# Attention and a gated long convolution on one core: scores of four heads per product, and values multiplied in 64-row halves

## The chip, the cores and the metric

The kernel runs on one core of a Trainium2 chip. The metric is the device time of one execution in microseconds; the median of the runs shown is compared. In the profile PE is TensorE (PEld its weight loads), DVE is VectorE, ACT is ScalarE, POOL is GpSimd and SP is SyncE, which here only issues transfers. Lines such as L691 are lines of the kernel before, unless the text says otherwise.

## What is computed

Eight batches, twelve heads, 448 positions, 64 features per head. Attention whose softmax has one more term in its denominator, then a projection into three parts, a circular convolution of the second part along the positions, a product of the three, and an output projection:

```python
scores = q @ k.T / sqrt(64)                     # per batch and head, 448 x 448
m = max(scores); e = exp(scores - m)
attn = e / (sum(e) + exp(-m) + 1e-09)           # the same as exp(s) / (sum(exp(s)) + 1)
x = (attn @ v).transpose(0, 2, 1, 3).reshape(8, 448, 768)
proj = x @ w_proj; x1, x2, x3 = three parts of 768
x2_conv = irfft(rfft(x2, axis=1) * rfft(filter, axis=0))
out = (x1 * x2_conv * x3) @ w_out               # 8 x 448 x 768, float32
```

All inputs are float32; the kernel multiplies in bf16 and sums in float32.

## The kernel before

**Two kinds of work.** For each batch there is attention (six pairs of heads) and then `dense(b)`: folding of x (`first`, `second`), the projection of the convolved part (`proj2`, L865), its spectrum by a small matrix of sines and cosines (`spectrum`, L892), the product with the filter's spectrum on VectorE (L906, L912), the two gates (`gate`, L938), the inverse transform (`inverse`, L977), unfolding and gating on VectorE, and the output projection (`project`, L1050). Attention of later batches is run between the pieces of dense work of earlier ones.

**An order made by a planner.** Nothing is emitted where it is written. Every piece is a task, added with an engine, a cost, a due time, what it needs, makes, takes and gives back. `Plan.run` imitates the engines and writes the tasks out in the order in which they would start; each engine then runs its own part of that order strictly in sequence. The due times come from the tables ATT, SLOT, DENSE, PACE, FOLD, LEAD, LOAD and others, so other tables give another order on every queue. The eight banks of PSUM are given out in the same way ("sc" and "op" take two neighbours, "hy" one). Where the plan leaves TensorE idle between 3 and 36 us it puts in filler products of zeros (L1136).

**Loads.** Four heads (a group, 24 in all) arrive together. `load_rows` (L372) reads keys or queries of four heads into 128 partitions: 64 partitions for each of two heads, seven successive positions in each partition, two such pairs beside each other. Values are read by `load_values` (L382) in four pieces of 64 partitions, so that two different blocks of seven stand under each other. `cast_rows` (L388) and `cast_values` (L393) turn them to bf16, on GpSimd save for the first group. The first two batches (`staged`) are transposed on TensorE (L437) and copied out of PSUM (L442); later ones (`loaded`) are transposed by a DMA on SP's queue (L483), keys and queries each by their own. There are six float32 rooms at first, then five.

**Scores and exponentials.** The 448 keys of a head are seven blocks of 64. A score task (`scores`, L655) makes four products, 64 keys by 448 queries on one quarter of the array each. For t = 1, 2, 3 the four are blocks t-1 and t+3 of two heads, so that one exponential (L666, 128 x 896) holds 128 keys of each head. Block 3 is left over; t = 0 puts block 3 of all four heads into one product, whose exponential goes into one of two buffers `er`; the other three use a ring of six buffers `e`. The first scores are single, then two are run together (`run`).

**Values.** The sum over keys for a pair of heads has two parts: `out_rests` (L683), eight products over 64 rows for block 3, and `out_rest` (L691), twelve products over 128 rows for each head. A column of ones beside the values gives the denominator. `out_rests` of pair j is emitted in the score run of the next pair. `norm` (L704 to L706) divides on VectorE and writes `xb`; `xb` is transposed to `xT` on TensorE in batch 0 (L779, L786, L788) and by DMA from batch 1 on (L770), four pairs and then two.

**Weights.** w_proj comes in on GpSimd's queue in its three parts (L631; the middle part in halves), the filter at L547 to L551, w_out at L636. They are asked for between the casts, in the planner's order.

The layout that the value products depend on:

```python
x = w_ if t else u ^ c                # which head's columns
j = t - 1 + 4 * c if t else 3         # which block of keys, on half c of the rows
```

## Time and profile before

| | |
|---|---|
| median of three runs | 393.48 us (392.73 to 393.92) |
| the profiled execution, by the timer | 388.91 us |
| its span in the profile | 387.1 us |
| TensorE granted clock, mean | 0.995 |
| scores, L655 | 672 products, 50.6 us busy |
| values over 128 rows, L691 | 1152 products, 44.6 us busy |
| values over 64 rows, L683 | 384 products, 14.2 us busy |
| gates, L938 | 576 products, 123.8 us busy |
| exponentials, L666 | 168, 147.7 us busy |
| SP's queue: value loads, L382 | 96, median 0.61 us to issue |

Busy time of a group is the union of its instructions; since a product takes some 0.19 us from start to end and the next starts long before that, the mean duration of one is not its price. The price is the distance between starts. The profiled execution's span stands below the median of the runs by 6.4 us, so sums are made against the span.

### The profile page before, as it was taken

The page shows a single profiled execution, that of the slowest core. Times are in us where ns is not written, and L with a number is a line of the kernel's source. Part 1 is how long each engine was busy: PE and PEld are TensorE (multiplying, and loading weights), DVE is VectorE, ACT ScalarE, POOL GpSimd, SP SyncE. Part 2 cuts the span into 40 slices and gives each one's busy share as a digit, 9 for nine tenths or more (in the row PEclk, how much of TensorE's full clock was granted, in tenths as well). Part 3 has the DMA queues.
Part 4 walks back from the last instruction along what each step waited for, and adds up shares of the span by engine and source line. Part 5 has one row for each costly group of instructions (what it writes and reads, how often), then busy time and mean ns, then how long its engine had stood idle before and what let it go on. Part 6 is the DMA issues. An engine that isn't in the chain of part 4 may idle for free.

```text
span 387.1 us, 9875 instructions
## 1 busy us (share of the span) xinstructions
PE 371.2 (96%) x3988; PEld 227.0 (59%) x3988; DVE 265.3 (69%) x651; ACT 263.7 (68%) x436; POOL 78.0 (20%) x97
## 2 busy tenths in 40 slices
PE   7989999999799999999999999999999999999995
PEld 4656755546555575555755456556665666657552
DVE  7388477893878838994489824986279745796480
ACT  4888777856756768866687576776677568634543
POOL 3832513140622323232222210000000000000000
PEclk9999999999989999999999999999999999999999
DMA  8999999999998999999988765220321012410204
GB/s 247 266 267 251 245 258 236 186 242 274 299 200 176 314 232 265 196 269 263 270 202 184 124 194 109 47 29 2 129 51 30 0 42 67 112 27 3 117 8 163
DMA packets 90862, 63.86 MB, mean 165 GB/s; under 512 B 58365, under 2 KB 87232, under 8 KB 90816
## 3 DMA queue, kind: packets, MB, share of 16 engines
q1 hardware_dynamic: 86064, 57.36, 59.6%
q0 software_dynamic: 4480, 5.41, 8.0%
q8 instruction: 31, 0.51, 0.5%
q10 hardware_dynamic: 272, 0.46, 0.3%
q14 instruction: 15, 0.12, 0.1%
HBM read 43.86 MB, written 11.01 MB: 142 GB/s over the span
## 4 chain that ended last, share of the span: by engine, by line
PE 74%; DVE 16%; DMA 6%; issue 2%; ACT 1%; POOL 0%; DVEq 0%
PE psum L938 22%; PE psum L865 16%; PE psum L1050 13%; PE psum L691 8%; PE psum L655 8%; DVE t L906 3%; DMA filt<-in_moe_filter_fft_dram 3%; PE psum L892 2%; PE psum L977 2%; PE psum L683 2%; DMA xT<-xb 2%; DVE xb L706 1%; DVE yh L912 1%; DVE g L953 1%; DMA nat<-in_q_dram 1%
## 5 line engine op out<-in xcount | busy, mean ns | idle before, releaser
L666 ACT ACTIVATE e<-psum 128x896 bf16<-128x896 f32 x144 | 125.7, 921 | 21.3 <-PE psum L655 20.7
L938 PE MATMUL psum<-xT,wproj_bf 128*128 128x448 bf16 x576 | 123.8, 355 | 0.1
L938 PEld LDWEIGHTS <-wproj_bf 128*128 128x128 bf16 x576 | 53.4, 98 | 46.3 <-issue 6.2
L865 PE MATMUL psum<-wproj_bf,xf 128*113 128x384 bf16 x384 | 70.2, 327 | 0.0
L865 PEld LDWEIGHTS <-xf 128*113 128x113 bf16 x384 | 49.2, 132 | 13.2 <-issue 1.4
L1050 PE MATMUL psum<-wout_bf,yT 128*128 128x384 bf16 x288 | 52.1, 326 | 2.4 <-DVE yT L1021 1.3
L655 PE MATMUL psum<-qT,kT 64*64 64x448 bf16 x672 | 50.6, 364 | 0.8 <-DVE xb L706 0.7
L953 DVE TENSOR_TENSOR g<-x,psum 128x448 bf16<-128x448 bf16 x48 | 29.5, 615 | 24.8 <-PE psum L938 24.6
L691 PE MATMUL psum<-vn,e 128*128 128x65 bf16 x1152 | 44.6, 194 | 0.0
L950 ACT CAST x<-psum 128x448 bf16<-128x448 f32 x48 | 25.7, 535 | 26.0 <-PE psum L938 25.6
L1062 ACT COPY osb<-psum 128x384 f32<-128x384 f32 x56 | 26.0, 484 | 22.2 <-PE psum L1050 21.8
L691 PEld LDWEIGHTS <-e 128*128 128x128 bf16 x1152 | 39.0, 97 | 2.7
L906 DVE TENSOR_TENSOR t<-xs,hrs 113x768 bf16<-113x768 bf16 (+1 forms) x64 | 37.4, 625 | 3.8 <-ACT xs L900 3.8
L1050 PEld LDWEIGHTS <-yT 128*128 128x128 bf16 x288 | 26.8, 98 | 22.1 <-issue 3.1
L704 DVE TENSOR_SCALAR rec<-psum 128x8 f32<-128x8 f32 x48 | 7.8, 162 | 39.4 <-PE psum L691 38.6
L706 DVE TENSOR_TENSOR xb<-psum,rec 128x512 bf16<-128x512 f32 x48 | 33.2, 691 | 1.7
L877 DVE CAST x<-psum 113x384 bf16<-113x384 f32 x32 | 17.7, 554 | 23.9 <-PE psum L865 23.8
L900 ACT CAST xs<-psum 113x384 bf16<-113x384 f32 (+1 forms) x64 | 28.2, 493 | 6.4 <-PE psum L892 5.8
L986 ACT CAST cr<-psum 128x452 bf16<-128x452 f32 x48 | 25.5, 548 | 9.1 <-PE psum L977 8.9
L388 POOL CAST nat<-nat 128x896 bf16<-128x896 f32 x22 | 22.6, 1028 | 41.2 <-DMA nat<-in_q_dram 17.4
L393 POOL CAST vn<-nat 128x896 bf16<-128x896 f32 x17 | 16.2, 954 | 71.9 <-DMA nat<-in_v_dram 56.6
L879 ACT CAST x<-psum 113x384 bf16<-113x384 f32 x32 | 15.4, 487 | 22.3 <-PE psum L865 22.3
(97 smaller groups left out, 381.0 us busy)
## 6 DMA issues: line engine op xcount, KB each, us to landing
out_dram<-osb SPq DMA_DIRECT2D x24, 384.0 KB, 2.6
nat<-in_k_dram SPq DMA_DIRECT2D x17, 448.0 KB, 4.9
nat<-in_q_dram SPq DMA_DIRECT2D x16, 448.0 KB, 5.5
nat<-in_v_dram SPq DMA_DIRECT2D x34, 128.0 KB, 4.6
nat<-in_v_dram SPq DMA_DIRECT2D x34, 96.0 KB, 4.5
wproj_bf<-in_moe_w_proj_dram POOLq DMA_DIRECT2D x2, 1152.0 KB, 15.5
k<-in_k_dram SPq DMA_DIRECT2D x4, 448.0 KB, 5.3
q<-in_q_dram SPq DMA_DIRECT2D x4, 448.0 KB, 5.2
```

Of the source, the lines that this page charges most:

```text
L655: nc.tensor.matmul(sc[64 * c : 64 * c + 64, u, 0:S], kT[b % 2][r, g, j, 64 * x : 64 * x + 64], qT[b % 2][r, g, :, 64 * x : 64 * x + 64],)
L666: nc.scalar.activation(e[:, 0 : 2 * S].rearrange("p (u n j) -> p u n j", u=2, j=7), pair(("sc", ("S", i, t)))[:, :, 0:S].rearrange("p u (j ...
L691: nc.tensor.matmul(out_bank(u)[:, n, :], P["e"][1 + t][:, u * S + n * 128 : u * S + n * 128 + 128], vn[b % 2][:, 2 * g + u, 4 * (u ^ w_) + ...
L706: nc.vector.tensor_tensor(W["xb", b][:, 2 * g : 2 * g + 2, :, 64 * w_ : 64 * w_ + 64], op[:, :, :, 0:DH], rec[:].unsqueeze(3).to_broadcast ...
L865: nc.tensor.matmul(pps[:FQ, :DCH], W["xf", b][:, pg, kt, 0:FQ], wproj_bf[:, kt, D + ch * DCH : D + (ch + 1) * DCH], start=(kt == 0), stop= ...
L900: nc.scalar.copy(L["xs", par, ch][:K, pg % 2, :], L["Z", pg, ch][:K, :DCH])
L906: nc.vector.tensor_tensor(t[:K], L["xs", par, ch][:K], h, op=ALU.mult)
L938: nc.tensor.matmul(p[:, :S], wproj_bf[:, kt, 2 * part * D + dt * 128 : 2 * part * D + (dt + 1) * 128], xT()[:, kt, 0:S], start=(kt == 0), ...
L950: nc.scalar.copy(L["x1", dt], p[:, :S])
L953: nc.vector.tensor_tensor(g[:, dt, :], L["x1", dt], p[:, :S], op=ALU.mult)
L1050: nc.tensor.matmul(ops[:n, :DCH], y[:, dt, 0:n], wout_bf[:, dt, ch * DCH : (ch + 1) * DCH], start=(dt == 0), stop=(dt == NDT - 1),)
L1062: nc.scalar.copy(L["os", st][:n, ch * DCH : (ch + 1) * DCH], L["O", st, ch][:n, :DCH])
```

## The change

What it does, in the new kernel:

- Scores: product j of a group holds block j of all four heads, for all seven j. The leftover buffers `er` are gone; there is one ring of eleven `e` buffers, and a group's seven are given back when both its value tasks are through.
- Values are loaded like keys (one transfer of 128 partitions), and stand by head on the two row halves.
- Values are multiplied over 64 rows: for a pair of heads 4 x 7 couples, one product on each row half, each half into its own bank. From the fourth group on such a task of 56 products is emitted in the score run that follows.
- Keys and queries share one tile; from batch 2 on they are transposed by one DMA. There are five rooms and two bf16 buffers for keys and queries.
- The first group's keys are cast by VectorE, not ScalarE; copies of transposed keys and of x in batch 0, and the mirror copies (L565, L566), are on VectorE alone.
- `xT` is transposed in halves of three pairs; the folds are of three and three.
- Many tables and some costs of the planner are other numbers, so the order on every queue differs. The filler in `spin` is other products.

The core of the diff:

```diff
-    EARLY1 = -19.08
-    ATT = [-9.51, 20.30, 77.88, 115.83, 86.04, 171.44, 197.84, 289.40]
-    SLOT = [4.14, 9.99, 5.26, 0.83, 1.75, 8.38, 8.43, 9.59]
-    DENSE = [53.55, 82.03, 128.26, 189.15, 232.32, 250.96, 315.14, 287.83]
-    PACE = [1.46, 2.48, 1.42, 1.15, 1.09, 3.10, 2.33, 6.50]
-    FOLD = [-28.99, -22.85, 7.59, -45.34, -22.73, 5.66, -21.16, 40.99]
-    BPS = 0.77
-    RE1 = 75.92
-    WT = 0.99
-    FT = 0.01
-    LEAD = [-15.44, 111.33, 32.83, 16.27, 78.96, 55.52, 15.28, 52.46]
-    VLATE = 0.94
+    SPIN = 38
+    EARLY0 = -7.81
+    EARLY1 = -31.53
+    NSINGLE, HOST = 22, 3
+    ATT = [61.68, 19.06, 51.44, 90.48, 134.71, 184.75, 265.58, 265.83]
+    SLOT = [7.18, 10.43, 5.20, 5.03, 0.93, 2.35, 4.65, 2.49]
+    DENSE = [32.35, 109.75, 123.73, 146.53, 223.55, 274.11, 331.19, 326.09]
+    PACE = [3.95, 1.73, 2.46, 3.56, 2.92, 2.20, 0.96, 1.78]
+    FOLD = [-33.07, 7.97, -54.75, 19.23, -27.96, -50.67, -61.51, -23.76]
+    BPS = -9.13
+    WT = 12.35
+    FT = -42.18
+    LEAD = [25.24, 37.06, -25.73, 55.99, 16.70, 47.21, -33.20]
+    VLATE = -3.09
     LOADS = ((1, 0), (1, 1), ("F", None), (0, None), (2, None), ("O", None))
-    LOAD = [14.88, 12.88, -21.39, 21.26, 41.09, 51.87]
+    LOAD = [19.70, 3.41, 13.35, 32.51, 35.06, 49.84]
     XALL = (1, 2, 3, 4, 5, 6, 7)
-    FOLD0 = [34.47, 92.42, 16.05]
+    FOLD0 = [47.70, 1.87, 54.60]
...
-    kT = [const.tile([128, NQ, 7, 128], BF16, name=f"kT{i}") for i in range(2)]
-    qT = [const.tile([128, NQ, 7, 128], BF16, name=f"qT{i}") for i in range(2)]
+    kqT = [const.tile([128, NQ, 2, 7, 128], BF16, name=f"kqT{i}") for i in range(2)]
     vn = [const.tile([128, NHP, 7, DH + 1], BF16, name=f"vn{i}") for i in range(2)]
 
-    es = [const.tile([128, 2 * S + REM], BF16, name=f"e{i}") for i in range(6)]
-    er = [const.tile([128, 2 * S + REM], BF16, name=f"er{i}") for i in range(2)]
-
-
-
-    ROOM = 7 * 128
-    nat = const.tile([128, 6 * ROOM], F32, name="nat")
-    k0 = const.tile([128, 2, ROOM], BF16, name="k0")
-    q0 = const.tile([128, 2, ROOM], BF16, name="q0")
-    kqn = nat[:, 0 : 3 * ROOM].bitcast(BF16).rearrange("p (x g c) -> p x g c", x=2, g=NQ)
-    stage = [nat[:, ROOM * i : ROOM * i + ROOM] for i in range(6)]
-    rooms = stage[3:] + [x.rearrange("p a c -> p (a c)").bitcast(F32) for x in (k0, q0)]
-
+    NE, NROOM, NNAT = 11, 5, 2
+    es = [const.tile([128, 2 * S + REM], BF16, name=f"e{i}") for i in range(NE)]
+    rooms = [const.tile([128, 7 * 128], F32, name=f"room{i}") for i in range(NROOM)]
+    kqn = [const.tile([128, 2, 7 * 128], BF16, name=f"kqn{i}") for i in range(NNAT)]
 
     plan = Plan(
         {
-            "e": 6, "er": 2, "k0": 2, "q0": 2, "u": 1, "w": 1, "xf": 1,
+            "e": NE, "kqn": NNAT, "u": 1, "w": 1, "xf": 1,
             "x2": 1, "xs": 2, "t0": 2, "t1": 2, "yh": 1, "g": 1, "x1": 2, "cr": 2, "cw": 1, "cv": 2, "yT": 1, "yR": 1,
...
-    def load_values(b, g, part, to):
-
-        lo, n, c, h, step, j = (
-            (0, 4, 0, 0, 3, 0), (4, 3, 0, 1, 1, 0), (0, 3, 1, 0, 3, 4), (3, 4, 1, 1, 1, 3),
-        )[part]
-        nc.sync.dma_start(
-            to[64 * c : 64 * c + 64].rearrange("p (w n) -> p w n", w=2)[:, :, lo * DH : (lo + n) * DH],
-            heads(v, b, 4 * g + h, step, j, n),
-        )
-
     def cast_rows(eng, to, src):
...
-            vn[b % 2][:, 2 * g : 2 * g + 2, :, 0:DH], src.rearrange("p (w t d) -> p w t d", w=2, t=7)
+            vn[b % 2][:, 2 * g : 2 * g + 2, :, 0:DH], src.rearrange("p (u j d) -> p u j d", u=2, j=7)
...
+    def arrive(b, g):
+        Q = b * NQ + g
+        at = tau(2 * Q)
+        staged = b < NSTAGED
+        old = [("V", 2 * Q - 2 * NHP), ("V", 2 * Q + 1 - 2 * NHP)] if b >= 2 else []
+        for m, (name, x) in enumerate((("k", k), ("q", q), ("v", v))):
+            n = 3 * Q + m
+            to = rooms[n % NROOM]
+            first = Q == 0 and name == "q"
+            lead = LEAD[2 * m : 2 * m + 2] if not staged else (
+                (EARLY0 if b == 0 else EARLY1) - 0.1 * m - (VLATE if m == 2 and b == 0 else 0),
+                (-1.0 if b == 0 else 4.0) if m == 2 else 5.0,
+            )
+            add("ACT" if first else "SP", 0.6 if first else 0.52, -21.0 if Q == 0 and m < 2 else at - lead[0],
+                lambda x=x, to=to, first=first: load_rows(nc.scalar if first else nc.sync, x, b, g, to),
+                need=[("c" + "kqv"[(n - NROOM) % 3], (n - NROOM) // 3)] if n >= NROOM else [],
+                make=[("s" + name, Q)], dma=1.35, run=1792)
+            if name == "v":
+                add("POOL", 0.96, at - lead[1], lambda to=to: cast_values(b, g, to), need=[("sv", Q)] + old,
+                    make=[("cv", Q)])
+                continue
+            eng = "DVE" if Q == 0 else "POOL"
+            def cast(m=m, to=to, eng=eng):
+                cast_rows(nc.vector if eng == "DVE" else nc.gpsimd, kqn[Q % NNAT][:, m], to)
+            add(eng, 0.56 if eng == "DVE" else 0.96, at - lead[1] + 0.01 * m, cast, need=[("s" + name, Q)], make=[("c" + name, Q)],
+                take=[("kqn", Q)])
+            if staged:
+                hy = ("hy", ("T" + name, Q))
+                def turn(m=m, hy=hy):
                     tb = bank2(hy)
                     for j in range(7):
                         c = slice(128 * j, 128 * j + 128)
+                        nc.tensor.transpose(tb[:, c], kqn[Q % NNAT][:, m, c], ident_bf)
+                on_act = False
+                def turned(m=m, hy=hy, on_act=on_act):
+                    (nc.scalar.copy if on_act else nc.vector.tensor_copy)(
+                        kqT[b % 2][:, g, m].rearrange("p j c -> p (j c)"), bank2(hy)[:, 0 : 7 * 128]
                     )
+                w = at - (3.5 if Q else 6.0)
+                add("PE", 0.45, w, turn, need=[("c" + name, Q), "ident"], make=[("T" + name, Q)], take=[hy],
+                    give=[("kqn", Q)])
+                add("ACT" if on_act else "DVE", 0.83 if on_act else 0.55, w + 0.1, turned, need=[("T" + name, Q)],
+                    make=[("kqT", Q)], give=[hy])
+        if not staged:
+            add("SP", 2.0, at - LEAD[6],
+                lambda: nc.sync.dma_start(
+                    kqT[b % 2][:, g].rearrange("p m j c -> p (m j) c"), kqn[Q % NNAT].rearrange("p m c -> p (m c)"),
+                    transpose=True,
+                ),
+                need=[("ck", Q), ("cq", Q), ("S", Q - 2 * NQ, 6)], make=[("kqT", Q)], give=[("kqn", Q)], dma=1.7, late=0.5)
...
-            nc.scalar.copy(fr[:].rearrange("p a b -> p (a b)"), rps[:FQ, 0 : 4 * FQ])
-            nc.scalar.mul(
-                fr[:, 1:3, :].rearrange("p a b -> p (a b)"), rps[:FQ, FQ : 3 * FQ], -1.0
+            nc.vector.tensor_copy(fr[:].rearrange("p a b -> p (a b)"), rps[:FQ, 0 : 4 * FQ])
+            nc.vector.tensor_scalar(
+                fr[:, 1:3, :].rearrange("p a b -> p (a b)"), rps[:FQ, FQ : 3 * FQ], -1.0, None, op0=ALU.mult
...
+    EX = {}
+    NU = 7 * NQ * n_batches
+    def scores(n):
+        Q, j = divmod(n, 7)
+        b, g = divmod(Q, NQ)
+        sc = pair(("sc", ("S", Q, j)))
+        for u in range(2):
+            r = slice(64 * u, 64 * u + 64)
+            for w in range(2):
+                c = slice(64 * w, 64 * w + 64)
+                nc.tensor.matmul(sc[c, u, 0:S], kqT[b % 2][r, g, 0, j, c], kqT[b % 2][r, g, 1, :, c])
+    def exps(n):
+        EX[n] = e = es[n % NE]
+        nc.scalar.activation(
+            e[:, 0 : 2 * S].rearrange("p (u n j) -> p u n j", u=2, j=7),
+            pair(("sc", ("S",) + divmod(n, 7)))[:, :, 0:S].rearrange("p u (j n) -> p u n j", j=7),
+            AF.Exp,
+            scale=SCALE,
+        )
+    def values(i):
+        Q, u = divmod(i, 2)
+        b, g = divmod(Q, NQ)
+        op = pair(("op", i))[:, :, 0 : NST * (DH + 1)].rearrange("p w (n d) -> p w n d", n=NST)
+        for n in range(NST):
+            for j in range(7):
+                for w in range(2):
+                    c = slice(64 * w, 64 * w + 64)
+                    nc.tensor.matmul(
+                        op[:, w, n, :],
+                        EX[7 * Q + j][c, u * S + n * 128 : u * S + n * 128 + 128],
+                        vn[b % 2][c, 2 * g + u, j, :],
+                        start=(n == 0 and j == 0),
+                        stop=(n == NST - 1 and j == 6),
+                    )
+    def value_args(i):
+        Q, u = divmod(i, 2)
+        return dict(
+            need=[("e", Q), ("cv", Q), ("ones", Q // NQ % 2), "pads"] + ([("V", i - 1)] if u else []), make=[("V", i)],
+            take=[("op", i)], give=[("e", 7 * Q + j) for j in range(7)],
+        )
+    def score_runs():
+        runs = [[n] for n in range(NSINGLE)]
+        runs += [list(range(n, min(n + 2, NU))) for n in range(NSINGLE, NU, 2)]
+        hosted = {}
+        for i in range(HOST * 2, 2 * NQ * n_batches):
+            Q, u = divmod(i, 2)
+            r = next(r for r, ns in enumerate(runs) if 7 * Q + 6 in ns) + 1 + u
+            if r < len(runs):
+                hosted[r] = i
+        for r, ns in enumerate(runs):
+            i = hosted.get(r)
+            a = value_args(i) if i is not None else dict(need=[], make=[], take=[], give=[])
+            def run(ns=ns, i=i):
+                for n in ns:
+                    scores(n)
+                if i is not None:
+                    values(i)
+            units = [divmod(n, 7) for n in ns]
+            add("PE", 0.2 + 0.155 * len(ns) + (1.0 if i is not None else 0.0), tau(2 * units[0][0], units[0][1] * 2 / 7), run,
+                need=[("kqT", Q) for Q, _ in units] + ([("run", r - 1)] if r else []) + a["need"],
+                make=[("S", Q, j) for Q, j in units] + [("run", r)] + a["make"],
+                take=[("sc", ("S", Q, j)) for Q, j in units] + a["take"], give=a["give"])
+            for n, (Q, j) in zip(ns, units):
+                add("ACT", 0.81, tau(2 * Q, j * 2 / 7) - 1.0, lambda n=n: exps(n), need=[("S", Q, j)], make=[("e", Q)],
+                    take=[("e", n)], give=[("sc", ("S", Q, j))])
+        for i in range(2 * NQ * n_batches):
+            if i not in hosted.values():
+                a = value_args(i)
+                add("PE", 1.1, tau(i // 2 * 2 + 2, 0.1 + 0.3 * (i % 2)), lambda i=i: values(i), need=a["need"], make=a["make"], take=a["take"],
+                    give=a["give"])
...
-                W["xb", b][:, 2 * g : 2 * g + 2, :, 64 * w_ : 64 * w_ + 64],
+                W["xb", b][:, hp].rearrange("p n (w d) -> p w n d", w=2),
...
+            if hp % 3 == 2:
+                ps = range(hp - 2, hp + 1)
+                add("SP", 1.8, w, x_dma, need=[("xb", NHP * b + h) for h in ps] + old,
+                    make=[m for h in ps for m in (("X", NHP * b + h), ("xT", b, h))], dma=1.7, late=0.5)
+        else:
...
-        for ds in (slice(0, 4), slice(4, 6)) if b else (slice(0, 2), slice(2, 4), slice(4, 6)):
+        for ds in (slice(0, 3), slice(3, 6)) if b else (slice(0, 2), slice(2, 4), slice(4, 6)):
...
-                add("POOL", 1.6, at, filter_load, need=["ft", "bps"], make=["filt"], take=[("yT", "F")], dma=4.1, run=1500, n=3, after=at)
+                add("POOL", 1.6, at, filter_load, need=["ft", "bps"], make=["filt"], take=[("yT", "F")], dma=4.4, run=3000, n=3, after=at)
-                add("POOL", 0.95, at, wout_load, make=["wout"], dma=6.9, run=1500, after=at)
+                add("POOL", 0.95, at, wout_load, make=["wout"], dma=6.0, run=3000, after=at)
-                add("POOL", 0.95, at, lambda part=part: wproj_load(part, None), make=[("w", part, 0), ("w", part, 1)], dma=6.9,
-                    run=1500, after=at)
+                add("POOL", 0.95, at, lambda part=part: wproj_load(part, None), make=[("w", part, 0), ("w", part, 1)], dma=6.4,
+                    run=3000, after=at)
-                add("POOL", 0.7, at, lambda part=part, ch=ch: wproj_load(part, ch), make=[("w", part, ch)], dma=3.5, run=1500, after=at)
+                add("POOL", 0.7, at, lambda part=part, ch=ch: wproj_load(part, ch), make=[("w", part, ch)], dma=3.0, run=3000, after=at)
```

## The prediction

> **What bounds the kernel now.** I read the page first, then the list of who waits for whom on TensorE, then the timeline of its value products, the start of the run, and one stretch of the middle. The page's first two parts and the groups:
>
> ```profile
> span 387.1 us, 9875 instructions
> ...
> PE 371.2 (96%) x3988; PEld 227.0 (59%) x3988; DVE 265.3 (69%) x651; ACT 263.7 (68%) x436; POOL 78.0 (20%) x97
> ...
> L655 PE MATMUL psum<-qT,kT 64*64 64x448 bf16 x672 | 50.6, 364 | 0.8 <-DVE xb L706 0.7
> L691 PE MATMUL psum<-vn,e 128*128 128x65 bf16 x1152 | 44.6, 194 | 0.0
> ```
>
> TensorE is busy 96% of the span; no other engine passes 69%. So the time is TensorE's work, plus the lead-in before it is saturated, plus its few waits. Those waits, from the list for TensorE alone:
>
> ```profile
> PE psum L892 <- DVE x L877: 2.0, 1, 2.0
> PE psum L1050 <- DVE yT L1021: 1.3, 2, 0.9
> PE psum L977 <- DVE xb L706: 0.9, 1, 0.9
> PE psum L1050 <- DVE g L953: 0.7, 1, 0.7
> ```
>
> All of them end on VectorE; no row names a DMA. The DMA engines are 80 to 90% busy until about 215 us in the page's slices, yet TensorE, which has other stages to run, does not wait for them. A cheaper load is therefore worth nothing by itself here.
>
> **Part 1, the value products.** This is what the change rewrites most. One pair of heads before, on TensorE's timeline:
>
> ```profile
> 205.03 0.57 PE L655 MATMUL psum<-qT,kT 64*64 64x448 bf16 x8
> 205.53 0.29 PE L683 MATMUL psum<-vn,er 64*128 64x65 bf16 x8
> 205.76 0.93 PE L691 MATMUL psum<-vn,e 128*128 128x65 bf16 x24
> 206.53 0.37 PE L977 MATMUL psum<-bt,yh 113*128 113x113 bf16 x4
> ```
>
> The starts give 0.23 us for the 8 products over 64 rows and 0.77 for the 24 over 128 rows, 1.00 us for a pair of heads, 48 times. The change makes it 56 products over 64 rows, in 28 couples on the two row halves. L683 is that very form. One of its products takes 0.193 us (mean), eight end after 0.29, so the last starts 0.10 after the first; that is three steps from couple to couple, about 33 ns each. The 128-row products step at (0.93 - 0.194) / 23 = 32 ns. So a couple costs what one 128-row product cost, and 24 + 4 = 28 of them were there before. After: 27 steps of 32 or 33 ns (0.86 to 0.89), plus 0.23 - 0.10 = 0.13 to leave the 64-row mode: 0.99 to 1.02 us. In place of 1.00 that is nothing to speak of: I take -0.3 us over the 48. The step of 33 is read from hundredths of a microsecond, so it may be 30 to 37: 0.94 to 1.13 per burst, -3 to +6 us. The 1152 more products and weight loads cost nothing only if they really run two abreast. The scores keep their number (672) and form, 0.50 us for eight. The order of the built program has 229 changes of array mode against 233, so nothing there.
>
> [...]
>
> **Part 2, the start.** Five rows of the timeline:
>
> ```profile
> 5.75 0.63 DVE L388 CAST q<-nat 128x896 bf16<-128x896 f32 x1 [0.89 <-DMA nat<-in_q_dram]
> 6.90 0.92 ACT L388 CAST k<-nat 128x896 bf16<-128x896 f32 x1
> 10.06 0.91 ACT L442 COPY kT<-psum 128x896 bf16<-128x896 bf16 x1 [2.24 <-PE psum L437]
> 11.34 0.57 PE L655 MATMUL psum<-qT,kT 64*64 64x448 bf16 x8
> 11.78 0.92 ACT L666 ACTIVATE er<-psum 128x896 bf16<-128x896 f32 x1 [0.81 <-PE psum L655]
> ```
>
> The first keys are cast late because ScalarE loads a table until 6.8. Now VectorE casts both: done by 5.75 + 2 x 0.63 = 7.0. The second set of seven transposes (0.93) ends at 7.9, its copy (0.62) at 8.6, ten filler products stand ahead of the scores, so scores start near 8.9 and the first exponential at 8.9 + (11.78 - 11.34) = 9.3, against 11.78: 2.4 us earlier. ScalarE also loses one cast (0.92), two copies (0.91 each), the mirror copies (0.54 + 0.36) and two copies of x; VectorE gains them, about 3.5 us, and from 11 to 36 us it has 6.6 us free (18.1 busy of 24.7). Without that cover, up to 3.5 us would show at the first projection (L865, 39.7 us).
>
> Half of the 2.4 is given back. Before, the exponentials of the second four heads follow the first without a gap (17.5 us). After, seven of eleven e buffers belong to one group of four heads until both its value bursts are through, and in TensorE's new order the first burst stands ahead of the next scores. Between the seventh exponential and the eighth lie 0.2 (semaphore), 1.0 (burst) and 0.44 (score to exponential): 1.6 us, twice before batch 0 is done, 3.2 in all. Before, ScalarE lost between 11.78 and 32.8 the waits 0.4, 0.2, 0.5, 0.7 and 0.5 and one copy of 0.9, 3.2 together. So the end of batch 0's exponentials gains 2.4 if nothing else goes wrong, and nothing if the new order also keeps the old small waits. I take -1.2; ends 0 and -2.4.
>
> The weights move too. On GpSimd's queue the load of the last third of w_proj, which the second gate of batch 0 reads, moves from behind the sixth keys' cast (issued at 43.1) to behind the fifth values' cast, 39.58 + 1.01 = 40.6 us; the first third moves back from 22.1 to behind the fifth keys' cast, about 32.2. These two took 11.2 and 19.8 us to land, 15.5 at the median. The last third is then in by 51.8 to 56.1; the gate that reads it starts at 55.8 before, some 54.6 after. I take no wait; up to +1.5.
>
> **Part 3, the loads.** Four value loads of 0.61 us of SP's issue time each become one of about 0.45, and two transposing loads (1.3 each) become one: some 3 us less of SP per four heads. SP waits 89 us for stores alone, so this is slack, and TensorE waits for no DMA: 0. GpSimd, which waits 56.6 us for values in order, would pass its casts on sooner. It matters only where attention is missing to fill TensorE.
>
> **Part 4, the middle.** The longest wait is in batch 1:
>
> ```profile
> 105.81 0.32 PE L892 MATMUL psum<-x,ft 113*112 113x384 bf16 x1 [2.01 <-DVE x L877]
> ...
> 107.00:110.00 3.00, 3.00 (x12) 1.00 (x14) 3.00 (x7) 0.22 (x1) 0.43 (x1) 0.50 1.25 228
> ```
>
> Six projection products, then at once the spectrum that needs VectorE's copy of them: TensorE stands for 2.0 us, and afterwards the granted clock is 0.50 for three microseconds; twelve gate products take 3.62 us on the chain where others take 2.27, another 1.35. In the new order a score pair and a value burst (0.5 + 1.0) stand between the last projections of batch 1 and their spectrum. They cover 1.5 of the 2.0, and likely part of the clock's dip: -2.0, ends 0 and -3.3. The other waits, some 5 us after the start, I leave as they are: the VectorE work behind them is the same, a third less or half more is possible (-2 to +3).
>
> **Sum.** -0.3 - 1.2 - 2.0 = -3.5 us on the profiled span of 387.1: 383.6. That execution took 388.9 us by the timer, and the runs shown have a median of 393.48, which is 6.4 above the span. The same difference gives 390.0 us, 0.9% less. A change under 0.3% (1.2 us) could not be told from none.
>
> **Rivals.** (A) TensorE does not keep couples abreast over 28 of them. For it: no burst here is longer than 8 such products, and 112 instructions must be fed in a microsecond, where the 24 of L691 and their loads are 48 in 0.77. Against it: 0.10 us for eight, and four score products that end together in 0.36. If each product took the 32 ns that a couple should, a burst is 55 x 32 + 130 = 1.89 us, +0.89 x 48 = +43 us: 433; halfway, 411. It decides from a step of 35 ns on: 27 x 2.7 ns x 48 = 3.5 us eats the gain. Chance 0.13 for slower by this. (B) The lead is lost and waits on VectorE grow: e buffers in one block of seven tie TensorE to ScalarE at each burst, 48 bursts in order behind an exponential (168 of 0.92). At 0.2 us for each in half of them it is +5, so 395 to 400, less any gain. Against it: L683 waited only 0.5 us for ScalarE in the whole run, with the same lag. Chance 0.20. (C) The early lead is absorbed, and batch 1 stalls elsewhere: 392.3 to 394.7, chance 0.12. (D) Batch by batch the waits on VectorE also go, another 5: 383 to 386, part of the faster side, 0.10. The forecast itself, 386 to 392, has 0.45. Faster 0.55, same 0.12, slower 0.33. The range 382 to 402 leaves out the far part of A.
>
> **What would show it.** Right: the value line near 1.0 us from a burst's first start to the next line's, its couples 32 or 33 ns apart; first exponential near 9.3; no 2 us wait at a spectrum in batch 1 and the clock at 1.00 there; TensorE busy about 370 us. Wrong: bursts of 1.1 us and more; gates waiting for w_proj near 54 us; rows in which TensorE waits for an exponential before the value products, or ScalarE for scores at each fourth group of heads.

## The result, and the profile after

The median after is 388.24 us (4 runs, 387.59 to 388.63) beside 393.11 before (4 runs, 391.44 to 393.92): a ratio of 0.988, with a 95% interval of 0.9843 to 0.9916. The change makes the kernel faster by 1.2%.

The profiled executions show less than that. The one after took 387.59 us by the timer, the lowest of its four runs, and has a span of 385.8. The one before took 388.91, which is 4.2 us under its median and 1.2 under the fastest of all the runs of it that were timed for this study (390.11). So the two traces differ by 1.3 us of span where the medians differ by 4.9 (the timer reads 1.8 us more than the span in both). What a comparison of the traces explains is therefore only a part; the rest had to come from experiments that are timed against the kernel before.

From the page of the kernel after, the span, the busy times, the clock by slices and the two groups that answer to L655 and L691 (with L683) of before:

```profile
span 385.8 us, 12193 instructions
...
PE 370.8 (96%) x5197; PEld 228.2 (59%) x5197; DVE 257.8 (67%) x658; ACT 258.9 (67%) x429; POOL 75.9 (20%) x100
...
PEclk9996999999999999999999999999999999999999
...
L616 PE MATMUL psum<-vn,e 64*128 64x65 bf16 x2688 | 51.5, 191 | 3.1 <-issue 2.6
L597 PE MATMUL psum<-kqT 64*64 64x448 bf16 x672 | 50.7, 368 | 1.3 <-DVE xb L674 0.9
```

TensorE is busy for 370.8 us (371.2 before), with 1209 more products. Two things are new: the value products have an idle time of 2.6 us ahead of them that ends on "issue", that is, on nothing the profile shows, and the fourth slice (29 to 39 us) has a granted clock of about 0.6.

The list of waits of TensorE after. Columns: total us, times, longest.

```profile
PE psum L616 <- issue: 2.6, 1, 2.6
PE psum L969 <- DVE yT L940: 2.5, 3, 2.0
...
PE psum L597 <- DVE xb L674: 0.9, 2, 0.6
PE psum L1055 <- issue: 0.8, 1, 0.8
```

The 2.0 us at a spectrum in batch 1, the longest wait of before, is gone; a wait of the same length stands now at an output projection (L969, at 84.7 us). TensorE's timeline over the same place after (start, duration, and in brackets the idle time before it):

```profile
101.03 1.06 PE L616 MATMUL psum<-vn,e 64*128 64x65 bf16 x56
102.02 0.37 PE L811 MATMUL psum<-x,ft 113*113 113x384 bf16 x1
...
105.58 0.57 PE L597 MATMUL psum<-kqT 64*64 64x448 bf16 x8
106.08 1.06 PE L616 MATMUL psum<-vn,e 64*128 64x65 bf16 x56
107.08 0.53 PE L811 MATMUL psum<-x,ft 113*112 113x384 bf16 x2
```

Two readings. From the first start of a value burst to the start of the next line is 1.00 us (107.08 - 106.08; the median of 46 bursts is 998 ns, and that of the L683 and L691 products together was also 998 ns). And a score pair with a burst stands ahead of the spectrum at 107.08, which does not wait.

The start, from the timelines of ScalarE and of TensorE:

```profile
8.80 5.78 ACT L601 ACTIVATE e<-psum 128x896 bf16<-128x896 f32 x7 [1.98 <-PE psum L597]
15.87 5.03 ACT L601 ACTIVATE e<-psum 128x896 bf16<-128x896 f32 x6 [1.30 <-PE psum L597]
```

```profile
20.88 0.27 PE L1055 MATMUL psum<-idle 128*128 128x128 bf16 x2 [0.79 <-issue]
...
23.86 0.90 PE L616 MATMUL psum<-vn,e 64*128 64x65 bf16 x45
27.35 0.35 PE L616 MATMUL psum<-vn,e 64*128 64x65 bf16 x11 [2.59 <-issue]
...
43.05 1.14 PE L784 MATMUL psum<-wproj_bf,xf 128*113 128x384 bf16 x6
```

The first exponential comes at 8.80 us in place of 11.78. But the fourth value burst is cut in two after 45 of its 56 products, for 2.59 us, and the first projection comes at 43.05 in place of 39.69. From there to the end it is 342.8 us, where it was 347.4: 4.7 us are won after the start, 3.4 are lost in it, and 1.3 remain. Of the 4.7, TensorE's waits after the first projection are 2.0 (4.6 in place of 6.6), its busy time 1.9 (334.4 in place of 336.3), and what follows its last product 0.8.

### The profile page after: what moved, and what is told of

Its sections match the earlier page's. It is cut to its first block, busy times and chain, and to the rows that moved or that the text cites. A ratio compares the mean times of both kernels' runs of the same rounds, so it can differ in the third digit from the quotient of the medians.

```text
span 385.8 us, 12193 instructions
## 1 busy us (share of the span) xinstructions
PE 370.8 (96%) x5197; PEld 228.2 (59%) x5197; DVE 257.8 (67%) x658; ACT 258.9 (67%) x429; POOL 75.9 (20%) x100
## 3 DMA queue, kind: packets, MB, share of 16 engines
q1 hardware_dynamic: 78192, 57.35, 57.3%
## 4 chain that ended last, share of the span: by engine, by line
PE 79%; DVE 14%; ACT 2%; issue 2%; DMA 1%; DVEq 0%; ACTq 0%
PE psum L857 24%; PE psum L784 15%; PE psum L969 13%; PE psum L616 10%; PE psum L597 9%; PE psum L811 2%; PE psum L896 2%; ACT e L601 2%; DVE t L825 2%; DVE xb L674 2%; DVE cv L925 1%; PE psum L410 1%; DMA room<-in_k_dram 1%; DVE g L872 1%; DVE cw L916 1%
## 5 line engine op out<-in xcount | busy, mean ns | idle before, releaser
L601 ACT ACTIVATE e<-psum 128x896 bf16<-128x896 f32 x168 | 145.9, 922 | 33.6 <-PE psum L597 32.3
L857 PE MATMUL psum<-xT,wproj_bf 128*128 128x448 bf16 x576 | 121.7, 352 | 0.6 <-DVE xb L674 0.6
L365 POOL CAST kqn<-room 128x896 bf16<-128x896 f32 x46 | 43.6, 950 | 105.3 <-DMA kqT<-kqn 51.4
L616 PEld LDWEIGHTS <-e 64*128 64x128 bf16 x2688 | 45.4, 94 | 19.8 <-issue 18.5
L616 PE MATMUL psum<-vn,e 64*128 64x65 bf16 x2688 | 51.5, 191 | 3.1 <-issue 2.6
L969 PE MATMUL psum<-wout_bf,yT 128*128 128x384 bf16 x288 | 51.5, 326 | 2.5 <-DVE yT L940 2.5
L597 PE MATMUL psum<-kqT 64*64 64x448 bf16 x672 | 50.7, 368 | 1.3 <-DVE xb L674 0.9
L969 PEld LDWEIGHTS <-yT 128*128 128x128 bf16 x288 | 27.1, 98 | 23.3 <-DVE yT L940 3.7
L825 DVE TENSOR_TENSOR t<-xs,hrs 113x768 bf16<-113x768 bf16 (+1 forms) x64 | 35.6, 595 | 6.4 <-ACT xs L819 6.3
L370 POOL CAST vn<-room 128x896 bf16<-128x896 f32 x24 | 23.4, 974 | 72.3 <-PE psum L616 54.6
```

Of the source, the lines that this page charges most:

```text
L365: eng.tensor_copy(to.rearrange("p (j u d) -> p u j d", u=2, j=7), src.rearrange("p (u j d) -> p u j d", u=2, j=7))
L597: nc.tensor.matmul(sc[c, u, 0:S], kqT[b % 2][r, g, 0, j, c], kqT[b % 2][r, g, 1, :, c])
L601: nc.scalar.activation(e[:, 0 : 2 * S].rearrange("p (u n j) -> p u n j", u=2, j=7), pair(("sc", ("S",) + divmod(n, 7)))[:, :, 0:S].rearran ...
L616: nc.tensor.matmul(op[:, w, n, :], EX[7 * Q + j][c, u * S + n * 128 : u * S + n * 128 + 128], vn[b % 2][c, 2 * g + u, j, :], start=(n == 0 ...
L825: nc.vector.tensor_tensor(t[:K], L["xs", par, ch][:K], h, op=ALU.mult)
L857: nc.tensor.matmul(p[:, :S], wproj_bf[:, kt, 2 * part * D + dt * 128 : 2 * part * D + (dt + 1) * 128], xT()[:, kt, 0:S], start=(kt == 0), ...
```

## The experiments

All are made from the kernel after or before by small edits, and the order of the other instructions stays, save in the one that plans the four pieces anew. A ratio is against runs of the kernel before on the same chip.

**Are the couples abreast?** The burst multiplies one row half after the other.

```diff
-        for n in range(NST):
-            for j in range(7):
-                for w in range(2):
+        for w in range(2):
+            for n in range(NST):
+                for j in range(7):
```

> The changed kernel with the 56 products of a value burst in another order: all 28 of one row half, then all 28 of the other, so that no two neighbours lie on different halves. Theory A (in the changed kernel couples run abreast, 32 ns for two, bound by the load of one set of weights): each product now takes about 32 ns, a burst 56 x 32 + 120 ns = 1.9 us in place of 1.00, and the time grows by 0.9 x 48 = 43 us less what was idle, to 425 to 432. Rival N (the step is set by the load of 128 columns whatever the row half, and the halves overlap through the queue anyway): burst near 1.0 to 1.2 us, time 388 to 398.

One run: 417.05 us, beside a median of 391.65 before. From its TensorE timeline:

```profile
203.09 1.84 PE L616 MATMUL psum<-vn,e 64*128 64x65 bf16 x56
204.85 1.18 PE L784 MATMUL psum<-wproj_bf,xf 128*113 128x384 bf16 x6
```

A burst now takes 1.76 us to the next line (median of 46: 1779 ns), 0.78 more. 48 bursts make 37 us; the run is 29 above the 388.24 of the kernel after. Of the 8 us between, the stops on "issue" give 3 (0.2 us are left) and the clock, now 1.00 from 11 to 36 us, some more; the rest wasn't followed, and this is a single run. In the kernel after, the two products of a couple start 3 ns apart, and couples 32 ns on average (33 at the median). So the pairing on two row halves is real, and it is what keeps 56 products at the price of 32 (998 ns where the other order takes 1779).

**What are the stops without a releaser?** Three kernels change the filler, which has no result. One leaves its 74 products out:

```diff
-    FILL = (3.0, 36.0, 0.6)
+    FILL = (3.0, 3.0, 0.6)
```

> The changed kernel without the 74 filler products of zeros that the planner puts between 3 and 36 us (148 instructions fewer on TensorE before the first projection; the rest of the order is the same). In the changed kernel TensorE stops for 2.6 us at 24.8 us, in the middle of its fourth value burst, with no instruction of another engine named; 256 instructions had begun since its stop of 0.8 us at 20.1, and a transfer of 16,384 bytes on the instruction queue begins at 25.0. Theory I (instruction supply: TensorE has used up what was fetched): the fourth burst now stands some 130 instructions earlier in the stream, so it ends before that supply runs out; no stop over 0.3 us without a releaser, the granted clock does not fall to half at 28 to 35 us, first projection (43.05 us) at 38 to 40, time 384 to 386. Rival W (a wait for data that the trace does not name): the stop stays within 0.3 us of its length at the same burst; time within 0.7 us of the changed kernel's 388.2. Rival C (the filler is needed for the clock): the stop is gone but TensorE runs at half clock for longer before 36 us; time 388 to 391.

388.65 us (12 runs), ratio 0.9907 (0.9879 to 0.9934). The list of waits and two stretches of time (PE busy, and PEclk, the granted clock):

```profile
PE psum L703 <- DVE xb L674: 3.5, 1, 3.5
PE psum L616 <- ACT e L601: 2.2, 4, 0.6
PE psum L597 <- ACT e L601: 1.9, 4, 0.6
```

```profile
11.30:36.00 24.70, 18.66 (x468) 12.37 (x467) 20.48 (x48) 18.27 (x23) 16.60 (x20) 0.93 1.12 313
36.00:60.00 24.00, 23.05 (x278) 15.42 (x279) 14.71 (x37) 15.73 (x29) 7.59 (x8) 0.93 1.12 260
```

No stop on "issue" is left, as theory I had it. But TensorE now waits for VectorE's `xb` and for exponentials, the clock still falls, to 0.93 in both stretches, the first projection comes at 42.75 us, where theory I had 38 to 40, and the time does not move. The other two kernels keep the filler and make it of fewer, wider products; one does it for the opening products too.

```diff
-            for _ in range(count):
-                nc.tensor.matmul(psum[:, 512 * i : 512 * i + 128], idle[:, 0:128], idle[:, 0:128])
+            for _ in range(max(1, round(count * 128 / 448))):
+                nc.tensor.matmul(
+                    psum[:, 512 * i : 512 * i + S], idle[:, 0:128], idle[:, 0:64].unsqueeze(1).to_broadcast([128, 7, 64])
+                )
```

> The changed kernel with its filler as products of 448 columns instead of 128, so many fewer that the columns are the same (74 become some 20 to 40), and its 82 opening products as 16 of 448 columns, as the kernel before has them: some 240 instructions fewer on TensorE before the fourth value burst, with TensorE kept as busy. Theory I: no stop without a releaser, no half clock after 12 us, first projection at 38 to 39.5 us, time 383.5 to 385.5, no worse than without filler. Rival W: the stop stays, 388.2 within 0.7.

> The kernel after, its fillers alone as products of 448 columns, about 21 for 74; the opening products stay. Instruction theory: stops between those of the kernel after (0.8 and 2.6 us) and those with both made wide (0.4 and 1.3): 386 to 388.5. If the number of instructions does not matter, the stops stay at 0.8 and 2.6 and the time at 388.2.

Both wide: 387.87 us (6 runs, 385.65 to 390.5), ratio 0.9896 (0.9846 to 0.9945); stops of 0.37, 1.33 and 0.83 us. Filler alone: 388.31 us (4 runs), ratio 0.9854 (0.9816 to 0.9893); one stop of 0.80 us at 34 us. The granted clock is 1.00 over the span of the profiled execution in both, and the first projection comes at 40.9 and 40.8 us, two earlier than after. The stops thus depend on the filler, and they can be had smaller. Yet neither kernel is shown to be faster than the one after. With the filler alone wide, the profiled execution has a span of 385.8 us again, so what its start wins is lost later; in the medians, two microseconds lie within the intervals.

The opposite test gives the kernel before the opening products of the kernel after, and splits its filler:

```diff
-                nc.tensor.matmul(psum[:, 512 * i : 512 * i + 128], idle[:, 0:128], idle[:, 0:128])
+                for c in range(2):
+                    nc.tensor.matmul(psum[:, 512 * i + 64 * c : 512 * i + 64 * c + 64], idle[:, 0:128], idle[:, 64 * c : 64 * c + 64])
```

> The kernel before, with the opening products of the kernel after (82 short ones for 16 of 448 columns) and each of its 83 filler products split into two of 64 columns: some 150 more products and as many weight loads in the first 33 us, for work that has no result. Instruction theory: TensorE stops with no releaser named at 15 to 30 us, 0.5 to 3 us in all, the granted clock falls after it, and the first projection comes 1 to 4 us after 39.7. Rival (the stops of the kernel after come from its value products or from its loads): no such stop, first projection at 39.5 to 40.2.

397.37 us (6 runs), ratio 1.0099 (1.0065 to 1.0133), and no stop on "issue" at all: the instruction theory, as a matter of their number, missed. The kernel is slower by 1% and its first projection late (42.4 us), but the waits name something else. The first of these stands much later, at 215 us; the second stands ahead of the first projection, and its longest is at 20.7 us:

```profile
PE psum L977 <- DVE xb L706: 4.0, 1, 4.0
PE psum L437 <- POOL k L388: 3.2, 2, 2.1
```

What sets it apart shows when the starts of products and weight loads are counted. In the kernels that stop, they stop at the same places in the count: after 705 and 961 instructions in the kernel after, in the one with values in two runs and in the one with two transposes (both below), after 449, 705 and 1985 with both wide, and after 1217 with the filler alone wide. These are 256 or multiples of it apart. The page has a queue of a kind of its own, and its transfers fit the count:

```profile
q8 instruction: 40, 0.66, 0.7%
```

40 transfers of 16,384 bytes, against 31 before; 16,384 bytes for 256 instructions would be 64 bytes each, and 40 times 256 is 10,240, of 10,394 products and weight loads (31 times 256 is 7,936, of 7,976 before).

So the count is taken as cut into blocks of 256 at these places, and the traces of all kernels here show how fast each block was used up. In the kernel after, the blocks that end in the two stops took 4.94 and 3.68 us. Of the blocks that TensorE enters in the first 65 us, in all kernels together, 17 were used up in 5.8 us or less, and each ends in a stop, of 0.2 to 2.6 us (the profile puts one of them, in the kernel with planned pieces, down to VectorE). The others took 6.0 us or more, and only one of them ends in a stop on "issue" (6.88 us, a stop of 0.32, in the kernel with halves below). The kernel without filler has none under 6.30 there, the kernel before with narrow products none under 6.13, the kernel before none under 7.20. So the stops go with the rate of the instructions, not with their number: a value burst is 112 of them in 998 ns. That a block is then used up before the next one has arrived is a reading of it, not shown.

The transfers agree with some 6 us. In the kernel after, TensorE enters a block at 14.93 us; the transfer begins at 18.35, and the block that follows starts at 20.88, after the stop. The next transfer begins at 25.00, 4.1 us after that, and TensorE goes on at 27.35. In both cases it goes on 2.4 to 2.5 us after a transfer has begun, 6.0 and 6.5 us after it entered the block before. Why the transfers begin only 3.4 and 4.1 us after a block is entered was not tried; the DMA engines are at 90% and more at that time, and at 266 us, where they are a third busy, a block used up in 4.67 us ends in no stop.

**Are loads slack?** The first kernel of this series loads values in four pieces of 64 partitions, as before, into the layout of after; the others take the two properties of such pieces apart. `load_pieces` is called in place of `load_rows` for values, at the same place in the order (only its body is shown):

```diff
+        for c in range(2):
+            for lo, n in ((0, 4), (4, 3)):
+                nc.sync.dma_start(
+                    to[64 * c : 64 * c + 64].rearrange("p (u n) -> p u n", u=2)[:, :, lo * DH : (lo + n) * DH],
+                    bass.AP(v.tensor, v[b, 4 * g + c].offset + lo * DH, [[7 * DH, 64], [2 * S * DH, 2], [1, n * DH]]),
+                )
```

> The changed kernel with each value load cut into four transfers of 64 partitions with runs of 1024 and 768 bytes, the shapes of the kernel before; nothing else differs, the planner's order neither. Theory O (what the middle gained, some 4 us of waits after the first projection, comes from the order): SP issues about 1.8 us more per four heads, time within 1 us of the changed kernel, 387.5 to 389.5. Rival L (the gain comes from cheaper loads): 2 to 4 us back, 390 to 392, with the waits on VectorE in the middle grown by as much.

404.6 us (4 runs), ratio 1.0311 (1.0267 to 1.0355): 16 us more than the kernel after, where "slack" had none. The same bytes arrive. Next, only the cut by partitions (two transfers of 64, full runs), and only the cut of the runs (two transfers of 128):

```diff
+        for c in range(2):
+            nc.sync.dma_start(
+                to[64 * c : 64 * c + 64].rearrange("p (u c) -> p u c", u=2),
+                bass.AP(v.tensor, v[b, 4 * g + c].offset, [[7 * DH, 64], [2 * S * DH, 2], [1, 7 * DH]]),
+            )
```

```diff
+        for lo, n in ((0, 4), (4, 3)):
+            nc.sync.dma_start(
+                to.rearrange("p (u n) -> p u n", u=2)[:, :, lo * DH : (lo + n) * DH],
+                bass.AP(v.tensor, v[b, 4 * g].offset + lo * DH, [[7 * DH, 128], [2 * S * DH, 2], [1, n * DH]]),
+            )
```

> The kernel after, with the values of each group loaded by two transfers of 64 partitions (runs of 1792 bytes, as before) in place of one of 128; the order of all else is unchanged. Values in four pieces (64 partitions, runs of 1024 and 768 bytes) took 404.6, 16.4 us more. Issue theory: what costs is SP's time, 0.61 us for each of three more issues; one more issue is a third of it, +5 us: 393 to 394. Run-length theory: what costs is the shorter runs (220 GB/s at 12 to 16 us with pieces, 334 without); full runs cost nothing: 387.5 to 389. Slack theory (the prediction): 387.5 to 389 as well.

> The kernel after, with the values of each group loaded by two transfers of 128 partitions, runs of 1024 and of 768 bytes; one more issue per group, as in the run with halves. Issue theory: the same as the halves, 393 to 394. Run-length theory: most of the 16.4 us of the four pieces, 398 to 405. Slack theory: 387.5 to 389.

Halves by partitions: 402.59 us (4 runs), ratio 1.0248 (1.0202 to 1.0295). Two runs: 389.73 us (10 runs), ratio 0.9921 (0.989 to 0.9953). The issue theory and the run-length theory missed both results, the slack theory missed the halves: one more issue and shorter runs cost 1.5 us together, 64 partitions instead of 128 cost 14 us. (The rate without pieces, from 12 to 16 us, is 364 GB/s in the trace, not the 334 of the first expectation.) The rows for the transfers that fill a room with values, by tile (ns min/median/max of the issue), one kernel after the other: after, halves, two runs.

```profile
L359 SPq DMA_DIRECT2D room<-in_v_dram x24: 367/406/2308, 1.3 to 208.8; - x24
```

```profile
L367 SPq DMA_DIRECT2D room<-in_v_dram x48: 595/608/1157, 1.3 to 224.1; - x48
```

```profile
L367 SPq DMA_DIRECT2D room<-in_v_dram x48: 367/471/1515, 1.3 to 210.9; - x48
```

And the main queue of after and of the halves (packets, MB, share of 16 engines' span):

```profile
q1 hardware_dynamic: 78192, 57.35, 57.3%
```

```profile
q1 hardware_dynamic: 78576, 57.36, 60.3%
```

A transfer of 64 partitions takes 0.61 us to issue where one of 128 takes 0.41 (medians), and the packets of the main queue take 60.3% of 400.4 us, 241 us per DMA engine, where it was 57.3% of 385.8, 221. Which of the two costs the time shows when the four kernels stand together. The third column is the sum of the issues of value loads in SP's queue, the fourth the time of the main queue's packets per engine:

| values of a group in | median, us | ratio | issues, us | packets, us |
|---|---|---|---|---|
| one of 128 partitions (after) | 388.24 | 0.988 | 15.2 | 221 |
| two of 128, shorter runs | 389.73 | 0.9921 | 30.1 | 226 |
| two of 64, full runs | 402.59 | 1.0248 | 31.1 | 241 |
| four of 64, shorter runs | 404.60 | 1.0311 | 63.3 | 241 |

Two transfers of 128 and two of 64 take SP's queue for the same time and differ by 13 us; four of 64 take it twice as long as two and cost 2 us more. So the time of the issues is not what costs. The packets go with the cost (that it comes about through them is argued, not shown): 18,176 packets of 1792 bytes are in the kernel after and in the one with halves, and they last 89 and 102 ns on average. Why they last longer with the halves no run shows. The rate of the DMA engines falls from 257 to 235 GB/s between 60 and 120 us.

Where the time goes shows in two stretches of after, and the same of the halves (columns: stretch, its length, then busy time and instructions of PE, PEld, DVE, ACT and POOL; last numbers: granted clock, DMA share, GB/s):

```profile
60.00:120.00 60.00, 56.98 (x869) 33.42 (x868) 44.14 (x107) 44.39 (x71) 19.01 (x20) 1.00 1.08 257
120.00:200.00 80.00, 79.39 (x1113) 47.86 (x1112) 54.87 (x143) 55.03 (x92) 18.28 (x19) 1.00 0.89 212
```

```profile
60.00:120.00 60.00, 54.36 (x844) 31.84 (x843) 39.44 (x97) 42.86 (x68) 19.19 (x19) 0.99 1.17 235
120.00:200.00 80.00, 72.45 (x946) 42.53 (x945) 50.26 (x126) 46.64 (x77) 17.97 (x19) 0.92 0.99 217
```

TensorE loses 2.6 us of work before 120 and 6.9 from there to 200, and the clock falls to 0.92. What it waits for there:

```profile
PE psum L865 <- DMA xT<-xb: 5.1, 1, 5.1
PE psum L904 <- DVE g L880: 3.6, 1, 3.6
```

L865 are the gates. Over the whole span TensorE's idle time grows by 9.0 us (24.0 against 15.0) and its busy time by 5.6 (376.4 against 370.8, at a mean granted clock of 0.977 against 0.991): together the 14.6 by which the spans differ. The transposes of `xT` stand in SP's queue behind the loads and the transposes of keys and queries: the one of the 5.1 us is issued at 138.8, right after a load of queries and a transpose that held the queue from 133.1 to 138.1, and lands at 145.9.

Then the planner is told of the four pieces, so that it can order the work for them:

```diff
...
+                for part in range(4):
+                    add("SP", 0.52, at - lead[0] + 0.02 * part, lambda to=to, part=part: load_piece(b, g, part, to),
+                        need=room, make=[("sv", Q)], dma=(0.45, 0.36)[part % 2], run=900)
...
```

> The four pieces of 64 partitions again, but the planner is told of them (four tasks of 0.52 us on SP, transfers of 0.45 and 0.36, runs of 900), so that the order of all queues is made for them. If the 16.4 us came only from an order that did not know of the pieces, this falls to 388 to 392. If the pieces themselves hold up the loads in the first 60 us, it stays at 396 to 406.

412.3 us (4 runs), ratio 1.0491 (1.0423 to 1.056): worse still, outside both ranges. An order that did not know of the pieces is not the cause; but the due times in the tables were left, so this is no measure of the best that such loads allow.

Last, the kernel before itself, once with slower and once with faster loads. Its keys in two halves by partitions:

```diff
+        for c in range(2):
+            eng.dma_start(
+                to[64 * c : 64 * c + 64].rearrange("p (u n) -> p u n", u=2),
+                bass.AP(x.tensor, x[b, 4 * g + c].offset, [[7 * DH, 64], [2 * S * DH, 2], [1, 7 * DH]]),
+            )
```

> The kernel before, with the keys of each group loaded by two transfers of 64 partitions (runs of 1792 bytes), order otherwise unchanged: one more issue of about 0.5 us on SP per group. If loads were slack in the kernel before, as the prediction had it, within 0.3% of 391.7. If SP's queue was short there too, +2 to +6 us; then the change's fewer issues are part of its gain.

407.7 us (4 runs), ratio 1.0387 (1.0332 to 1.0441), 14 us slower, far beyond both ranges. The kernel before had no slack in its loads either. And its values in one transfer:

```diff
-            add("SP", 0.52, want + 0.02 * part, lambda part=part: load_values(b, g, part, to), need=need,
+            add("SP", 0.52, want + 0.02 * part, lambda part=part: load_rows(nc.sync, v, b, g, to) if part == 0 else None, need=need,
```

> The kernel before, with the values of each group loaded by one transfer of 128 partitions, as keys are, in place of four of 64; order unchanged. The values then stand at other rows than the value products take them for, so the output is not the reference's; the work is the same otherwise. If the speed of loads holds the kernel before up (theory L), it gains what the change gains by its loads: -2 to -8 us (385 to 391 beside 393). If its order cannot use faster loads, or loads are slack there (prediction), within 0.3%.

386.87 us (4 runs, 385.85 to 387.54), ratio 0.982 (0.9792 to 0.9848): 6.6 us faster. This one part, put into the kernel before, is worth at least what the whole change is worth (0.9843 to 0.9916). In its profiled execution (span 385.4) the first projection comes at 38.3 us, the packets of the main queue take 221 us per engine where they took 231, SP's transfers take 108 of the first 200 us to issue where they took 162, and the rate of the DMA engines between 4 and 12 us is 386 GB/s where it was 285. Which of these the gain comes by was not taken apart in this kernel. First the row of before, then of this run:

```profile
4.00:12.00 8.00, 6.20 (x60) 5.47 (x61) 4.24 (x13) 4.02 (x6) 3.34 (x5) 1.00 1.10 285
```

```profile
4.00:12.00 8.00, 6.00 (x65) 5.29 (x65) 4.18 (x13) 4.31 (x6) 3.50 (x5) 1.00 1.06 386
```

**One transpose for keys and queries.** The kernel after with two:

```diff
-                lambda: nc.sync.dma_start(
-                    kqT[b % 2][:, g].rearrange("p m j c -> p (m j) c"), kqn[Q % NNAT].rearrange("p m c -> p (m c)"),
-                    transpose=True,
-                ),
+                lambda: [
+                    nc.sync.dma_start(kqT[b % 2][:, g, m], kqn[Q % NNAT][:, m], transpose=True) for m in range(2)
+                ],
```

> The kernel after, with the transposing transfer of keys and queries from batch 2 on as two transfers (18 more on SP's queue). If one transpose for both is a part of the gain, +1 to +5 us. If it is slack, as the prediction had it, 387.5 to 389.5.

387.12 us (4 runs, 385.37 to 389.16), ratio 0.9831 (0.9788 to 0.9874). One transpose in place of two is no part of the gain. Nor does it free SP's queue: the one takes 3.05 us to issue (median of 18) where the two of before took 1.31 and 1.26. If anything two are faster, but the interval meets that of the kernel after, so this, like both wide fillers, isn't shown to beat it.

## Why the prediction was right, and where it was not

The forecast, faster at 390.0 us with 0.55 for faster, holds: 388.24. The way to it is only partly right; two of the four parts failed, one of them the most important.

**Part 1, value products: right.** A burst costs 998 ns, forecast 0.99 to 1.02; couples step by 32 to 33 ns, as forecast; TensorE's busy time is 370.8, forecast about 370. Rival A has the price it was given when couples are undone (1.78 us a burst, forecast 1.89), but it did not come about. Its doubt about feeding 112 instructions in a microsecond was not idle: one burst of the traced execution stops for 2.59 us, at a block's end, and the others do not. The 56 products of a burst take 998 ns, 18 ns each.

**Part 2, the start: right up to the first exponentials, the term of -1.2 failed.** The first exponential comes at 8.80 (forecast 9.3), the seventh and eighth are 1.30 us apart (forecast 1.6). Two steps failed. The first is "the end of batch 0's exponentials gains 2.4 if nothing else goes wrong": that end is 34.07 us, 32.76 before, since TensorE stopped at two ends of blocks for 0.8 and 2.6 us and the clock fell to 0.86 between 11 and 36 us. Without filler, and with the filler alone wide, it is 30.34 and 30.17: there the 2.4 are gained.

The second is that the first projection would follow. In these two kernels it comes at 42.75 and 40.82 all the same, later than the 39.69 of before, because TensorE waits 3.5 and 2.2 us for `xb`. In VectorE's order, which is that of the kernel after, folds of x stand ahead of the division: in the trace of after they take it from 34.05 to 37.65 us, without a pause. The prediction named this danger ("Without that cover, up to 3.5 us would show at the first projection") and put nothing in the sum for it. Whether the work taken over from ScalarE or the new order holds VectorE up was not separated. In place of -1.2 the first projection measured +3.4.

That no gate waits for weights was right, its steps were not: the last third of w_proj was issued at 33.33 us (forecast 40.6) and took 20.4 us to land, at 53.69 (forecast 11.2 to 15.5); the first third landed at 44.35, and the first gate at 56.39 did not wait.

**Part 3, the loads: failed.** "SP waits 89 us for stores alone, so this is slack, and TensorE waits for no DMA: 0." Both readings are true (the list has waits for ScalarE too, 1.6 and 0.5 us, but none of TensorE's products for a DMA), and the conclusion is wrong. The rows of before, DMA engines by slices of 9.7 us SP's longest wait, and SP's longest wait of the first 200 us:

```profile
DMA  8999999999998999999988765220321012410204
```

```profile
SPq L1069 <- ACT osb L1062: 89.4, 13, 20.7
```

```profile
SPq L483 <- POOL nat L388: 16.4, 11, 8.5
```

Whole loads of values alone are worth 6.6 us in the kernel before; half of the values' partitions per transfer cost the kernel after 14 us. SP's 89 us of waiting for stores all lie after 200 us in the trace of before, where hardly a load is left; until then issuing alone took 162 of SP's 200 us, and the DMA engines were busy for 80% and mostly over 90% of the time (the prediction noted 80 to 90). And a late load does not stop TensorE under its own name: with halves the largest waits are called `xT` (5.1 us) and VectorE (3.6). That the delay goes from the load through a cast on GpSimd, attention and `xb` to a transposing transfer in the same queue is argued from the order, not followed link by link. What the prediction priced as issue time, 3 us of SP per four heads, is 2 (the joined transpose saves none), and in the kernel after the time of the issues is not what costs, as the four kernels show; it didn't see that the transfers to 64 partitions are slower ones (with them the queue's 1792-byte packets last 102 ns on average, without them 89).

**Part 4, the middle: right in kind, too small.** The 2.0 us wait and the clock of 0.50 are gone, and the score pair and the burst now stand there. TensorE's waits after the first projection fell by 2.0 us in all, from 6.6 to 4.6, though a single one as long stands now at an output projection. From the first projection to the end the profiled execution is 4.7 us shorter, where -2.0 and -0.3 were forecast. How much of the other 2.4 is the new order and how much the earlier loads is not separated.

**The sum** was right by luck. On the profiled span -3.5 us were forecast (383.6) and -1.3 measured (385.8). The 6.4 us that were added for the median are 1.8 between timer and span and 4.6 by which the profiled execution of before happened to be faster than the median shown; after, both together are 2.4. The two errors, 2.2 too low and 4.0 too high, leave 390.0 beside 388.24. In the mechanism two errors cancel as well: the start that was counted as a gain is none, and the loads that were counted as nothing are worth, in the kernel before, as much as the whole gain. Whether the parts of the change other than the loads win or lose anything by themselves is not settled: the intervals of the kernel before with whole loads and of the kernel after just touch. What the 64-row value products do is to make such a load usable: a layout by head on two row halves needs no block of another head under it, at the same 998 ns. Also open is what the kernel before does in its usual executions that its profiled one, 4.2 us under the median, does not show.

## What to carry to other kernels

Transfers to 64 partitions cost 14 us here, in the kernel after (402.59 beside 388.24) as in the one before (407.7 beside 393.24), though they moved the same bytes in the same runs; lay data out so that each transfer covers all 128, and rearrange the multiplication for it where that costs nothing, as here (998 ns a burst before and after). "TensorE waits for no DMA" does not make loads slack: look whether the DMA engines are full in the stretch in question (80% and mostly over 90% here), and try it by making one load slower. A gain at the start counts only if what feeds the rest of the run comes earlier too: here the exponentials came 3.0 us earlier (8.80 in place of 11.78) and the first projection 3.4 later.

## What the runs showed of the hardware

- Two 64-row products on the two row halves start 3 ns apart, the next couple 32 to 33 ns after the first, over a whole burst of 56.
- In five kernels (after, values in two runs, two transposes, both fillers wide, filler alone wide) TensorE stops on nothing that the profile shows after 449, 705, 961, 1217 or 1985 products and weight loads, 256 or a multiple of it apart; the instruction queue moved 40 transfers of 16,384 bytes where there were 10,394 of these in the kernel after, and 31 for the 7,976 of before. In the first 65 us, with the DMA engines 80% busy and mostly more, all 17 blocks of 256 that were used up in 5.8 us or less end in a stop of 0.2 to 2.6 us; of those that took 6.0 us or more, one does. After the stops of the kernel after the granted clock is about 0.6 in one slice (0.86 between 11 and 36 us). At 266 us a block used up in 4.67 us ends in no stop.
- The same 448 KB per group in two transfers of 64 partitions rather than one of 128 took the DMA engines 241 us of packets in place of 221, with the same number of 1792-byte packets (102 ns on average in place of 89), and each took 0.61 us to issue in place of 0.41; the run took 402.59 us in place of 388.24. Two transfers of 128 partitions took SP's queue as long and cost 1.5 us where these cost 14.
- One transposing transfer of keys and queries took 3.05 us to issue where two took 1.31 and 1.26.
